# Linear attention and a top-2 expert layer in one kernel: the attention steps are put in another order, and each expert's weights are fetched in one burst

## The chip, the cores and the metric

The kernel runs on one core of a Trainium2 chip. The metric is the time on the device in microseconds (us), the median of several executions. In the text PE is TensorE (matrix products), DVE is VectorE, ACT is ScalarE, POOL is GpSimd and SP is SyncE. Each engine runs its own instructions strictly in program order and waits for the others by semaphores. POOL issues nearly all transfers here: those that convert 32-bit floats to bf16 on the way, and the indirect ones, which take a list of row numbers.

## What is computed

The reference has two parts. The first is linear attention on 8 batches of 8 heads with 576 positions of 64 numbers; the second is a layer of 8 experts that sees the 4608 outputs of the first as rows of 512 numbers.

```python
# attention, for every batch and head
phi = lambda x: np.where(x > 0, x, np.exp(x) - 1.0) + 1.0
q_p, k_p = phi(q), phi(k)
kv  = einsum('bhsd,bhse->bhde', k_p, v);   z = k_p.sum(axis=2)
num = einsum('bhsd,bhde->bhse', q_p, kv);  den = einsum('bhsd,bhd->bhs', q_p, z)[..., None] + 1e-6
x = (num / den)                            # to (4608, 512): the 8 heads of a position in one row

# router: two experts for each row
noisy = x @ w_gate + log1p(exp(x @ w_noise)) * noise        # (4608, 8)
top2, top2_w = the two largest of noisy in each row, and their softmax

# experts: w1[e] is 512 x 1024, w2[e] is 1024 x 512
for e in range(8):
    out[rows of e] += top2_w * (relu(x[rows of e] @ w1[e]) @ w2[e])
```

All inputs are 32-bit floats in HBM (q, k and v have 9.4 MB each, the experts' weights 33.6 MB); so is the output (9.4 MB).

## The kernel before

The batches are worked in four groups `g` of two. For each group there are loads of k, v and q, then these steps:

```python
def exp(self, g, t):               # ACT: two instructions, 128 x 2304 each
def phi(self, g, t, *parts):       # DVE: part 0 is max(x,0)+1 in place, parts 1 and 2 take the minimum with exp
def kv_mm(self, g, h):             # PE: half of k_p' v and of k_p' 1, into two tiles of ps_misc
def kv_ev(self, g, h):             # DVE: those two tiles to SBUF, masked
def kv_b1(self, g), kv_b2(self, g) # PE and ACT: kv times the router's weights, so that the logits come with num
def qt(self, g, *parts):           # PE transposes of q_p, ACT copies them out (5 parts)
def num(self, g, t):               # a third of the group: 3 of its 9 columns of rows
    ...                            # PE: dl = denominators and logits (24 small matmuls)
    ...                            # DVE: rden = 1/(den + 1e-6)
    for i in range(3):             # PE: num;  DVE: xr[g % 2] = num * rden (bf16 rows)
        ...
    ...                            # DVE: lwt = logits * rden
```

Routing works on a *unit*: some of the 9 columns of 128 rows of one group. Its three steps are chains of small DVE instructions, and a unit must have been counted before the next is placed (`carry` counts the rows that each expert has got). Dispatch then writes each finished row of 1152 bytes into the region of each of its two experts in HBM, one indirect transfer of 128 rows at a time.

```python
UNITS = [(0, 0, 3), (0, 3, 6), (0, 6, 9), (1, 0, 9), (2, 0, 9), (3, 0, 3), (3, 3, 9)]   # (group, first column, end)

def rt_a(self, u):                 # logits: sum lwt over the 8 heads, then softplus on ACT
    nc.vector.tensor_reduce(out=r["lg"], in_=_ap(self.lwt[:, c0], [[128, n], [1, 16], [16, 8]]), op=ALU.add, axis=AX.X)
    nc.scalar.activation(out=r["sp"], in_=r["lg"][:, :, 8:16], func=ACT.Exp)
    nc.scalar.activation(out=r["sp"], in_=r["sp"], func=ACT.Ln, bias=1.0, scale=1.0)
def rt_b(self, u): ...             # 15 DVE instructions: the two largest of 8; PE: ranks of the rows in each expert
def rt_c(self, u): ...             # 13 and more DVE instructions: softmax, row numbers posi, carry
def dispatch(self, u, a=0, z=9):
    for ci in range(c0 + a, min(c1, c0 + z)):
        for sl in range(2):
            self.nc.gpsimd.indirect_dma_start(out=self.x_sorted, out_offset=...posi[:, ci - c0, sl]..., in_=self.xr[g % 2][:, ci, :]...)
```

The order of the calls in `attention()` is the order on every engine. The middle of it, and its end:

```python
    for g, u in ((1, 3), (2, 4)):
        n = g + 1
        pa.exp(n, "q")
        pa.num(g, 0)
        pa.num(g, 1)
        pa.kv_mm(n, 0)
        pa.phi(n, "q")
        pa.num(g, 2)
        pa.kv_mm(n, 1)
        pa.kv_ev(n, 0)
        pa.rt_a(u)
        pa.kv_ev(n, 1)
        pa.kv_b1(n)
        pa.qt(n, 0)
        pa.rt_b(u)
        pa.kv_b2(n)
        if g == 1:
            pa.exp(3, "k")
            pa.phi(3, "k", 0)
        pa.rt_c(u)
        pa.qt(n, 1, 2, 3, 4)
        pa.dispatch(u, 0, 4)
        if g == 1:
            pa.load(3, "q")
        pa.dispatch(u, 4, 9)
        if g == 1:
            pa.phi(3, "k", 1, 2)
            pb.w_tiles(1)
            pb.w_load(1, 0, 1, 2, 3)
    # then the loads of expert 0's first rows (xt), num(3, ...), units 5 and 6, and the first products of expert 0
```

Buffers that set the order: three for k and q together (`A_kq`), two for v, two for exp (`A_e`), three PSUM tiles `ps_misc` for all of kv_mm, kv_b1, kv_b2 and qt, one PSUM tile `dl`, and two for the rows, `xr[g % 2]`.

The expert part takes the up to 1216 rows of an expert in blocks of 512, 512 and 192. While `mm1` of one block runs (rows times w1, relu), `mm2` of the block before (times w2), its gating and its output follow. A row that is the second visit of its token reads what the first visit wrote (gather), adds, and is written out (scatter), so the gather of a new expert waits until all scatters of the expert before have landed.

```python
    def interval(self, cur, prev, weights=()):
        ...                         # mm1(cur) in turn with mm2(prev, t) and scatter(prev, t)
        if cur and new and not cur["first"]:
            self.gather(cur)        # first block of an expert: behind the last scatter of the one before
        for e, i in weights:
            self.w_load(e, i)       # a quarter of an expert's weights: 1 MB of HBM, 0.5 MB of SBUF
# the loop over the blocks: two quarters in each interval until all are there
        loads = [(e, i) for e in range(2, E) for i in range(4)]
            todo, loads = loads[:2], loads[2:]
```

Of the kernel before, what the change touches and what calls it, by code (L numbers as in the profile page):

```python
# [15 lines left out]
P = 128  # L16
# [9 lines left out]
UNITS = [(0, 0, 3), (0, 3, 6), (0, 6, 9), (1, 0, 9), (2, 0, 9), (3, 0, 3), (3, 3, 9)]  # L26

ROUNDS = [(3, 512), (4, 768)]
# [76 lines left out]
class PhaseA:  # L105
# [36 lines left out]
    def exp(self, g, t):  # L142
        self.e[g, t] = self.ep.tile([P, 4, 9, P], BF16, name="e")
        for two in range(2):
            e, x = self._views(g, t, two)
            self.nc.scalar.activation(out=e, in_=x, func=ACT.Exp)  # L146
# [115 lines left out]
    def rt_a(self, u):  # L262
# [6 lines left out]
        nc.vector.tensor_reduce(  # L269
            out=r["lg"], in_=_ap(self.lwt[:, c0], [[128, n], [1, 16], [16, 8]]), op=ALU.add, axis=AX.X)  # L270
# [302 lines left out]
def attention(pa, pb, c, x_sorted, zrow):  # L573

    nc = pa.nc

    pa.exp(0, "k")
    pa.phi(0, "k")
    nc.vector.memset(zrow[:], 0.0)
    for e in range(E):  # L580

        for r0, n in ((1024, P), (1152, P)):
            nc.sync.dma_start(out=x_sorted[e * REGION + r0 : e * REGION + r0 + n, :], in_=zrow[0:n])
    pa.load(1, "q")
    pa.kv_mm(0, 0)
    pa.kv_ev(0, 0)
    pa.kv_mm(0, 1)
    pa.kv_ev(0, 1)
    pa.kv_b1(0)
# [3 lines left out]
    pa.qt(0, 0, 1, 2, 3, 4)  # L593
    pa.load(2, "k")
    pa.load(2, "v")
    pb.w_tiles(0)
    pb.w_load(0, 0, 1, 2, 3)
    pa.exp(1, "k")
    pa.num(0, 0)
    pa.rt_a(0)  # L600
    pa.phi(1, "k", 0)
    pa.rt_b(0)
    pa.phi(1, "k", 1)
    pa.rt_c(0)
    pa.dispatch(0)
    pa.num(0, 1)
    pa.rt_a(1)
    pa.phi(1, "k", 2)
    pa.rt_b(1)
    pa.kv_mm(1, 0)  # L610
    pa.rt_c(1)
    pa.dispatch(1)
    pa.load(2, "q")
    pa.exp(1, "q")
    pa.num(0, 2)
    pa.rt_a(2)
    pa.kv_ev(1, 0)
    pa.rt_b(2)
    pa.kv_mm(1, 1)
    pa.phi(1, "q", 0)  # L620
    pa.rt_c(2)
    pa.dispatch(2)
    pa.kv_ev(1, 1)
    pa.kv_b1(1)
    pa.phi(1, "q", 1, 2)
    pa.qt(1, 0)
    pa.kv_b2(1)
    pa.qt(1, 1, 2, 3, 4)
    pa.load(3, "k")
    pa.load(3, "v")  # L630
    pa.exp(2, "k")
    pa.phi(2, "k")
    for g, u in ((1, 3), (2, 4)):
        n = g + 1
        pa.exp(n, "q")
        pa.num(g, 0)
        pa.num(g, 1)
# [3 lines left out]
        pa.kv_mm(n, 1)  # L641
        pa.kv_ev(n, 0)
        pa.rt_a(u)
        pa.kv_ev(n, 1)
        pa.kv_b1(n)
        pa.qt(n, 0)
        pa.rt_b(u)
        pa.kv_b2(n)
        if g == 1:
            pa.exp(3, "k")  # L650
            pa.phi(3, "k", 0)
        pa.rt_c(u)
        pa.qt(n, 1, 2, 3, 4)
        pa.dispatch(u, 0, 4)
        if g == 1:
            pa.load(3, "q")
# [127 lines left out]
```

## Time and profile before

| what | value |
|---|---|
| median of 3 executions | 558.66 us (547.3 to 565.68) |
| span of the profiled execution | 556.6 us |
| busy: PE, DVE, ACT, POOL | 358.6, 214.2, 157.8, 266.9 us |
| transfers issued by POOL: share of the 16 engines' span | 56.4% (69.90 MB) |
| transfers issued by SP and ACT | 17.2% (12.68 MB) |
| read from HBM and written to it | 79.83 MB, 32.90 MB |
| dispatches, scatters, gathers (indirect, POOL) | 72, 80, 70, each about 1 us of POOL |

A page cuts the span into 40 slices of 13.9 us and gives each engine's busy share in tenths. A second part follows the chain of work that ended last backwards from the end. Other views list, for a stretch of time, the instructions of one engine with the idle time before each and what ended it, or count who waited for whom.

### The profile page before, as it was taken

How to read it: one execution, taken by the hardware profiler on the slowest of the kernel's cores; microseconds unless marked ns; L12 is line 12 of the kernel's file. 1: busy time of each engine (PE TensorE's matmuls, PEld its weight loads, DVE VectorE, ACT ScalarE, POOL GpSimd, SP SyncE). 2: the span in 40 equal slices, each digit the busy share in tenths (PEclk: the TensorE clock that was granted, in tenths of full speed). 3: DMA queues.
4: the chain of work that ended last, by engine and by line, in shares of the span. 5: the costliest groups of instructions: out<-in, count | busy, mean ns of one | idle time of the engine just before them, and what ended most of it. 6: DMA issues, size and time to landing. Idle time of an engine off the chain costs nothing.

```text
span 556.6 us, 7359 instructions
## 1 busy us (share of the span) xinstructions
PE 358.6 (64%) x2783; PEld 202.7 (36%) x2811; DVE 214.2 (38%) x548; ACT 157.8 (28%) x272; POOL 266.9 (48%) x289
## 2 busy tenths in 40 slices
PE   0432343562443127569999999359949975999980
PEld 0432332452333113324454454224424442454440
DVE  1438773856193166123335152023224233235130
ACT  2163318061222004113324324103402411424310
POOL 6023373006725613724585376068348474564660
PEclk9996555555556558969999999859969997999995
DMA  9999969202892331396499899969979794573640
GB/s 145 221 248 212 228 147 213 50 2 75 191 162 76 117 81 52 117 188 133 105 223 165 161 217 165 118 110 224 166 149 229 187 196 129 95 228 117 187 145 13
DMA packets 95311, 83.34 MB, mean 150 GB/s; under 512 B 58741, under 2 KB 81269, under 8 KB 95264
## 3 DMA queue, kind: packets, MB, share of 16 engines
q0 software_dynamic: 40448, 69.90, 56.4%
q1 hardware_dynamic: 53152, 12.68, 17.2%
q10 hardware_dynamic: 1664, 0.18, 0.4%
q8 instruction: 24, 0.39, 0.3%
q14 instruction: 23, 0.19, 0.1%
HBM read 79.83 MB, written 32.90 MB: 203 GB/s over the span
## 4 chain that ended last, share of the span: by engine, by line
PE 49%; DVE 14%; issue 13%; another core or an unknown queue 7%; ACT 7%; DMA 6%; POOL 2%; POOLq 0%; DVEq 0%; ACTq 0%
PE b L483 22%; PE b L472 21%; ACT e L146 4%; DVE e L156 3%; PE misc L170 2%; DMA out_dram<-y,si 2%; DVE xr L248 2%; PE num L226 2%; DMA kq<-in_q_dram 2%; DMA kq<-in_k_dram 2%; ACT pqt L219 1%; DVE kq L153 1%; DVE y L487 1%; DVE lwt L254 1%
## 5 line engine op out<-in xcount | busy, mean ns | idle before, releaser
L483 PE MATMUL b<-w,hT 128*128 128x512 bf16 (+1 forms) x624 | 156.5, 392 | 24.4 <-DVE y L487 23.0
L472 PE MATMUL b<-xt,w 128*128 128x512 bf16 (+3 forms) x756 | 149.5, 341 | 23.5 <-ACT hT L474 11.4
L474 ACT ACTIVATE hT<-b 128x512 bf16<-128x512 f32 (+3 forms) x192 | 95.5, 508 | 227.0 <-PE b L472 167.5
L487 DVE SCALAR_TENSOR_TENSOR y<-b,gate,L 128x512 f32<-128x512 f32 x70 | 50.8, 743 | 184.4 <-issue 64.6
L355 POOL DMA_INDIRECT x_sorted<-xr,posi x72 | 71.6, 994 | 104.2 <-ACT pqt L219 51.9
L497 POOL DMA_INDIRECT out_dram<-y,si x80 | 79.1, 989 | 63.1 <-DVE y L487 22.3
L472 PEld LDWEIGHTS <-w 128*128 128x128 bf16 x768 | 73.8, 100 | 95.7 <-issue 32.3
L455 POOL DMA_INDIRECT L<-out_dram,gi x70 | 71.2, 1016 | 73.9 <-DMA out_dram<-y,si 52.7
L483 PEld LDWEIGHTS <-hT 128*128 128x128 bf16 (+1 forms) x640 | 64.0, 102 | 97.3 <-issue 34.8
L226 PE MATMUL num<-kvbd,pqt 128*64 128x128 bf16 x288 | 21.3, 302 | 44.3 <-DVE xr L248 35.8
L226 PEld LDWEIGHTS <-pqt 128*64 128x64 bf16 x576 | 24.1, 156 | 70.4 <-issue 67.8
L146 ACT ACTIVATE e<-kq 128x2304 bf16<-128x2304 bf16 x16 | 33.0, 2124 | 31.7 <-issue 22.4
L446 DVE MEMSET L<- 128x512 f32 x70 | 34.0, 485 | 4.2 <-ACT hT L474 0.3
L170 PE MATMUL misc<-v,e 64*128 64x128 bf16 x288 | 19.5, 305 | 23.3 <-DVE e L156 19.6
L170 PEld LDWEIGHTS <-e 64*128 64x128 bf16 x576 | 20.2, 124 | 26.5 <-DVE e L156 19.6
L248 DVE TENSOR_TENSOR xr<-num,rden 128x512 bf16<-128x512 f32 x36 | 24.0, 689 | 15.0 <-remote 6.2
L153 DVE TENSOR_SCALAR kq<-kq 128x4608 bf16<-128x4608 bf16 x8 | 11.0, 1370 | 39.0 <-ACT e L146 39.0
L217 PE MATMUL misc<-ident,e 128*128 128x128 bf16 x144 | 16.9, 312 | 13.6 <-DVE e L156 10.7
L226 PE MATMUL dl<-kvbd,pqt 128*64 128x34 bf16 x288 | 11.1, 215 | 21.1 <-issue 12.3
L156 DVE TENSOR_TENSOR e<-e,kq 128x2304 bf16<-128x2304 bf16 x16 | 21.2, 1360 | 0.2
L490 DVE TENSOR_SCALAR y<-b,gate 128x512 f32<-128x512 f32 (+1 forms) x10 | 7.5, 750 | 34.4 <-PE b L483 19.0
L301 PE MATMUL dl<-A,ut 128*128 128x24 bf16 (+2 forms) x7 | 1.3, 190 | 29.4 <-DVE A L297 23.8
(91 smaller groups left out, 196.9 us busy)
## 6 DMA issues: line engine op xcount, KB each, us to landing
w<-in_moe_w_dram POOLq DMA_DIRECT2D x32, 512.0 KB
kq<-in_k_dram POOLq DMA_DIRECT2D x8, 576.0 KB
v<-in_v_dram POOLq DMA_DIRECT2D x8, 576.0 KB
kq<-in_q_dram POOLq DMA_DIRECT2D x8, 576.0 KB
x_sorted<-zrow SPq DMA_DIRECT2D x16, 144.0 KB
out_dram<-y,si POOLq DMA_INDIRECT x80
x_sorted<-xr,posi POOLq DMA_INDIRECT x72
L<-out_dram,gi POOLq DMA_INDIRECT x70
```

What stands on the lines that cost most here:

```text
L146: self.nc.scalar.activation(out=e, in_=x, func=ACT.Exp)
L156: nc.vector.tensor_tensor(out=e, in0=e, in1=x, op=ALU.min)
L170: nc.tensor.matmul(out=ps[j][:, i, cols], lhsT=e[half, hp, ci, :], rhs=r, start=(i == 0 and ci == 0 and rhs == "v"), stop=(i == 1 and ci = ...
L226: self.nc.tensor.matmul(out=out[half], lhsT=self.pqt[g, ci][:, hp, half], rhs=self.kvbd[g][:, j, hp, cols], start=start, stop=stop, skip_g ...
L248: nc.vector.tensor_tensor(out=_ap(xr[:, ci, 0:HD], [[64, 4], [256, 2], [1, 64]]), in0=_ap(ps, [[128, 4], [64, 2], [1, 64]]), in1=_ap(rden[ ...
L355: r = self.nc.gpsimd.indirect_dma_start(out=self.x_sorted, out_offset=bass.IndirectOffsetOnAxis(ap=self.r["posi", u][:, ci - c0, sl : sl + ...
L455: r = nc.gpsimd.indirect_dma_start(out=b["L"][t][0:m].bitcast(INT32), out_offset=None, in_=self.out.bitcast(INT32), in_offset=bass.Indirec ...
L472: nc.tensor.matmul(out=ps[:, 0:n], lhsT=w1[:, dc, fc * P : fc * P + P], rhs=b["xt"][:, dc, 0:n], start=(dc == 0), stop=(dc == 3))
L474: nc.scalar.activation(out=b["hT"][:, fc, 0:n], in_=ps[:, 0:n], func=ACT.Relu)
L483: nc.tensor.matmul(out=ps[0:m], lhsT=b["hT"][:, fc, t * P : t * P + m], rhs=w2[:, fc, :], start=(fc == 0), stop=(fc == 7))
L487: nc.vector.scalar_tensor_tensor(out=y[0:m], in0=ps[0:m], scalar=gate[0:m, tt : tt + 1], in1=b["L"][t][0:m], op0=ALU.mult, op1=ALU.add)
L497: r = nc.gpsimd.indirect_dma_start(out=self.out, out_offset=bass.IndirectOffsetOnAxis(ap=si[0:m, tt : tt + 1], axis=0), in_=b["y", t][0:m] ...
```

## The change

It is meant to let POOL, which issues every dispatch one after the other, start on them earlier, and to keep the weights out of the way of the transfers that an expert's beginning waits for. The parts are these.

1. **Units.** Groups 0, 1 and 2 are one routing unit of 9 columns each (group 0 was three units of 3); group 3 is 6 + 3 columns (it was 3 + 6). There are five units in place of seven.
2. **Dispatch directly behind its routing.** In the loop, rt_b, rt_c and the dispatch follow each other; the transposes `qt` that were in between come ahead of them or behind.
3. **Exponentials and loads ahead of need.** exp(1, k) starts before the transposes of group 0; exp(3, k) comes before the last transposes; the loads of q for groups 2 and 3 are issued well ahead of their exponentials (load(3, q) stood in the middle of a dispatch).
4. **The sum over the heads** in rt_a is three additions by halves in place of one strided reduction.
5. **The zero rows** that mark unused places are half as many, and come later.
6. **Weights in one burst.** All four quarters of the weights of expert e + 2 are loaded in the first interval of expert e, in place of two quarters in each of the first twelve intervals.

The diff, cut:

```diff
--- before.py
+++ after.py
@@ -23,9 +23,9 @@
 CAP = 1216
 T_CAP = 10
 
-UNITS = [(0, 0, 3), (0, 3, 6), (0, 6, 9), (1, 0, 9), (2, 0, 9), (3, 0, 3), (3, 3, 9)]
-
-ROUNDS = [(3, 512), (4, 768)]
+UNITS = [(0, 0, 9), (1, 0, 9), (2, 0, 9), (3, 0, 6), (3, 6, 9)]
+
+ROUNDS = [(1, 512), (2, 768)]
 REGION = N_TOK
 ROW_W = 576
 BIG = 1.0e6
... (exp takes parts, as phi does)
@@ -266,8 +267,11 @@
         tile_ = lambda name, shape, dt=FP32: self.rt.tile([P] + shape, dt, name=name)
         r = self.r
         r["lg"], r["sp"] = tile_("lg", [9, 16])[:, 0:n], tile_("sp", [9, E])[:, 0:n]
-        nc.vector.tensor_reduce(
-            out=r["lg"], in_=_ap(self.lwt[:, c0], [[128, n], [1, 16], [16, 8]]), op=ALU.add, axis=AX.X)
+
+        lw = lambda a, z: self.lwt[:, c0:c1, a:z, :]
+        for k in (4, 2):
+            nc.vector.tensor_tensor(out=lw(0, k), in0=lw(0, k), in1=lw(k, 2 * k), op=ALU.add)
+        nc.vector.tensor_tensor(out=r["lg"], in0=self.lwt[:, c0:c1, 0, :], in1=self.lwt[:, c0:c1, 1, :], op=ALU.add)
         nc.scalar.activation(out=r["sp"], in_=r["lg"][:, :, 8:16], func=ACT.Exp)
         nc.scalar.activation(out=r["sp"], in_=r["sp"], func=ACT.Ln, bias=1.0, scale=1.0)
 
@@ -573,92 +577,84 @@
 def attention(pa, pb, c, x_sorted, zrow):
 
     nc = pa.nc
-
     pa.exp(0, "k")
     pa.phi(0, "k")
-    nc.vector.memset(zrow[:], 0.0)      # and 16 transfers of 128 zero rows
     pa.load(1, "q")
     pa.kv_mm(0, 0)
+    pa.kv_mm(0, 1)
     pa.kv_ev(0, 0)
-    pa.kv_mm(0, 1)
     pa.kv_ev(0, 1)
+    pa.load(2, "v")
     pa.kv_b1(0)
     pa.kv_b2(0)
     pa.exp(0, "q")
     pa.phi(0, "q")
-    pa.qt(0, 0, 1, 2, 3, 4)
     pa.load(2, "k")
-    pa.load(2, "v")
-    pb.w_tiles(0)
-    pb.w_load(0, 0, 1, 2, 3)
-    pa.exp(1, "k")
+    pa.exp(1, "k", 0)
+    pa.qt(0, 0, 1)
+    pa.exp(1, "k", 1)
+
     pa.num(0, 0)
+    pa.qt(0, 2, 3, 4)
+    pa.phi(1, "k")
+    pa.load(2, "q")
+    pa.num(0, 1)
+    pa.kv_mm(1, 0)
+    pa.num(0, 2)
+    pa.kv_mm(1, 1)
+    nc.vector.memset(zrow[:], 0.0)
+    ...                                # 8 transfers of 128 zero rows, 8 of the marks of 64 rows
     pa.rt_a(0)
-    pa.phi(1, "k", 0)
+    pa.kv_ev(1, 0)
+    pa.kv_ev(1, 1)
+    pa.exp(1, "q")
+    pa.kv_b1(1)
     pa.rt_b(0)
-    pa.phi(1, "k", 1)
+    pa.phi(1, "q", 0)
     pa.rt_c(0)
-    pa.dispatch(0)
-    pa.num(0, 1)
-    pa.rt_a(1)
-    pa.phi(1, "k", 2)
-    pa.rt_b(1)
-    pa.kv_mm(1, 0)
-    pa.rt_c(1)
-    pa.dispatch(1)
-    pa.load(2, "q")
-    pa.exp(1, "q")
-    pa.num(0, 2)
-    pa.rt_a(2)
-    pa.kv_ev(1, 0)
-    pa.rt_b(2)
-    pa.kv_mm(1, 1)
-    pa.phi(1, "q", 0)
-    pa.rt_c(2)
-    pa.dispatch(2)
-    pa.kv_ev(1, 1)
-    pa.kv_b1(1)
+    pa.load(3, "v")
+    pa.dispatch(0, 0, 4)
     pa.phi(1, "q", 1, 2)
+    pa.load(3, "k")
+    pa.dispatch(0, 4, 9)
     pa.qt(1, 0)
     pa.kv_b2(1)
-    pa.qt(1, 1, 2, 3, 4)
-    pa.load(3, "k")
-    pa.load(3, "v")
+    pa.qt(1, 1)
     pa.exp(2, "k")
-    pa.phi(2, "k")
-    for g, u in ((1, 3), (2, 4)):
-        n = g + 1
+    pa.qt(1, 2, 3, 4)
+    for g in (1, 2):
+        n, u = g + 1, g
         pa.exp(n, "q")
         pa.num(g, 0)
+        pa.phi(n, "k")
+        if g == 1:
+            pa.load(3, "q")
+            pb.w_tiles(0)
+            pb.w_load(0, 0, 1, 2, 3)
         pa.num(g, 1)
         pa.kv_mm(n, 0)
         pa.phi(n, "q")
         pa.num(g, 2)
         pa.kv_mm(n, 1)
+        pa.qt(n, 0, 1)
+        pa.rt_a(u)
         pa.kv_ev(n, 0)
-        pa.rt_a(u)
         pa.kv_ev(n, 1)
         pa.kv_b1(n)
-        pa.qt(n, 0)
+        pa.qt(n, 2)
+        pa.kv_b2(n)
         pa.rt_b(u)
-        pa.kv_b2(n)
+        pa.rt_c(u)
+        pa.dispatch(u)
         if g == 1:
-            pa.exp(3, "k")
-            pa.phi(3, "k", 0)
-        pa.rt_c(u)
-        pa.qt(n, 1, 2, 3, 4)
-        pa.dispatch(u, 0, 4)
-        if g == 1:
-            pa.load(3, "q")
-        pa.dispatch(u, 4, 9)
-        if g == 1:
-            pa.phi(3, "k", 1, 2)
             pb.w_tiles(1)
             pb.w_load(1, 0, 1, 2, 3)
+            pa.exp(3, "k")
+        pa.qt(n, 3, 4)
 
     col = c["rowpos"]
     r1, r2 = pb.block(0, 0, 512, "r1", 0, True), pb.block(0, 512, 256, "r2", 0, True)
@@ -667,19 +663,20 @@
     pb.meta_load("r2", 512, 2, "read1")
     pb.xt_load(r2, "read1")
     pa.num(3, 0)
-    pa.rt_a(5)
     pa.num(3, 1)
-    pa.rt_b(5)
-    pa.rt_c(5)
-    pa.dispatch(5)
+    pa.rt_a(3)
     pa.num(3, 2)
-    pa.rt_a(6)
-    pb.mm1(r1, 0, 1, 2, 3)
-    pa.rt_b(6)
-    pb.mm1(r1, 4, 5)
-    pa.rt_c(6)
-    pa.dispatch(6)
-    pb.mm1(r1, 6, 7)
+    pa.rt_b(3)
+    pa.rt_c(3)
+    pa.dispatch(3)
+    pb.mm1(r1, 0)
+    pa.rt_a(4)
+    pb.mm1(r1, 1, 2)
+    pa.rt_b(4)
+    pb.mm1(r1, 3, 4)
+    pa.rt_c(4)
+    pa.dispatch(4)
+    pb.mm1(r1, 5, 6, 7)
     pb.meta("r1", c["cnt"][0][:], col[:, 0:4], code_of(0))
     pb.interval(r2, r1)
     pb.meta("r2", c["cnt"][1][:], col[:, 4:6], code_of(0))
@@ -731,7 +728,6 @@
         blocks = [pb.block(0, 768, CAP - 768, 0, 6, True)]
         for e in range(1, E):
             blocks += [pb.block(e, r, n, e, r // P) for r, n in ((0, 512), (512, 512), (1024, CAP - 1024))]
-        loads = [(e, i) for e in range(2, E) for i in range(4)]
         pb.meta_load(0, 0, T_CAP)
         pb.xt_load(blocks[0])
         for i, b in enumerate(blocks):
@@ -743,10 +739,10 @@
             if i == 0 or b["e"] != blocks[i - 1]["e"]:
                 e = b["e"]
                 pb.meta(e, c["carry"][:, e : e + 1], c["rowpos"][:], code_of(e))
-            todo, loads = loads[:2], loads[2:]
-            for e, part in todo:
-                if part == 0:
-                    pb.w_tiles(e, 1 if e < 6 else 0)
+            todo = []
+            if e + 2 < E and (i == 0 or b["e"] != blocks[i - 1]["e"]):
+                pb.w_tiles(e + 2, 1 if e + 2 < 6 else 0)
+                todo = [(e + 2, part) for part in range(4)]
             pb.interval(b, prev, todo)
             prev = b
         pb.interval(None, prev)
```

## Prediction

> **What bounds the kernel now.** I read the page's slices first, then POOL's instructions in order of time over the attention, then the chain of waits, then who waited for whom in the expert part, and last the busy time in one stretch per expert. The slices, of 13.9 us each:
>
> ```profile
> PE   0432343562443127569999999359949975999980
> DVE  1438773856193166123335152023224233235130
> POOL 6023373006725613724585376068348474564660
> PEclk9996555555556558969999999859969997999995
> DMA  9999969202892331396499899969979794573640
> ```
>
> Two halves with different limits. Up to slice 17 no engine is full: PE seldom over half, at half its clock, DVE full in single slices, the DMA engines full only to slice 6. That is a chain of waits, not an engine at its peak. From slice 18 PE is at 9 with holes at slices 25, 26 and 29, and the DMA engines are full up to slice 29 and not after. The next view is POOL's timeline; the columns are start, duration, instruction and, in brackets, its idle time just before and who ended that:
>
> ```profile
> 86.14 0.75 POOL L132 DMA_DIRECT2D kq<-in_k_dram  x1
> ...
> 127.73 2.09 POOL L355 DMA_INDIRECT x_sorted<-xr,posi  x1 [37.68 <-ACT pqt L219]
> ...
> 138.72 1.48 POOL L132 DMA_DIRECT2D kq<-in_q_dram  x2
> ...
> 170.90 1.03 POOL L355 DMA_INDIRECT x_sorted<-xr,posi  x1 [14.26 <-ACT pqt L219]
> ...
> 205.45 0.95 POOL L355 DMA_INDIRECT x_sorted<-xr,posi  x1 [11.99 <-issue]
> ...
> 220.80 0.96 POOL L355 DMA_INDIRECT x_sorted<-xr,posi  x1 [8.07 <-ACT hT L474]
> ```
>
> These are the first dispatches of groups 1 (127.73), 2 (170.90) and the two units of group 3. Inside a group they follow each other every 1.26 us, so group 2 and 3 with 36 dispatches need 45.5 us of POOL; they took 170.9 to 235.7, so 20 us of POOL waited for routing (11.99 + 8.07). Before that POOL stood 37.68 us with nothing to send. Between 127.73 and 138.72 stand eight dispatches ahead of the load of q for group 3, and its exponential waits for that load: "ACT e L146 <- issue: 22.4, 1, 22.4" in the list of waits, from 126.9 to 149.4.
>
> The expert part, POOL again, and then the busy time from each expert's first gather to the next (experts 1 to 6; columns: stretch, its length, busy us of PE, PEld, DVE, ACT, POOL with instruction counts, granted clock, share of the DMA engines, GB/s):
>
> ```profile
> 340.10 1.57 POOL L396 DMA_DIRECT2D w<-in_moe_w_dram  x2
> 341.97 1.04 POOL L497 DMA_INDIRECT out_dram<-y,si  x1 [0.30 <-DVE y L487]
> 343.32 0.96 POOL L497 DMA_INDIRECT out_dram<-y,si  x1 [0.30 <-issue]
> 364.61 1.04 POOL L455 DMA_INDIRECT L<-out_dram,gi  x1 [20.33 <-DMA out_dram<-y,si]
> ```
>
> ```profile
> 270.80:313.60 42.80, 42.27 (x212) 20.51 (x215) 12.94 (x26) 15.25 (x31) 25.19 (x26) 1.00 1.06 183
> 313.60:364.60 51.00, 39.51 (x203) 19.50 (x206) 12.74 (x26) 14.28 (x29) 24.88 (x26) 0.92 1.05 157
> 364.60:409.00 44.40, 36.34 (x173) 17.64 (x176) 12.66 (x26) 12.02 (x24) 25.03 (x27) 0.88 1.02 174
> 409.00:443.30 34.30, 30.05 (x141) 14.53 (x144) 12.66 (x26) 9.53 (x19) 23.24 (x24) 0.87 0.88 193
> 443.30:478.90 35.60, 26.65 (x131) 13.04 (x133) 12.53 (x26) 7.91 (x18) 19.98 (x21) 0.90 0.58 136
> 478.90:513.10 34.20, 33.90 (x174) 16.66 (x176) 12.54 (x26) 11.75 (x24) 19.86 (x21) 1.00 0.65 170
> ```
>
> Experts 1 to 3, with six quarters of weights each, take 42.8, 51.0 and 44.4 us; expert 4 with four and experts 5 and 6 with none take 34.2 to 35.6. The excess is the boundary: two quarters were queued just ahead of the last two scatters, so these land late and the next gather stands 10.75, 20.33 and 13.58 us, against 3.62, 2.21 and 2.17 us at the last three boundaries.
>
> **What the Trainium skill says.** "DMA: Bandwidth & Descriptors", section "Issuing engines are not separate DMA queues": all issuing engines' transfers run on the same 16 DMA engines and interleave. The trace agrees: POOL's own transfers take 56.4% of them and those of SP and ACT 17.2%, and a scatter that lands in about 2 us alone took 20 us behind weights. The same page, "Two DMAs through the same engine are not ordered": a transfer that reads what an earlier one wrote has to wait for its completion; that is the gather's wait, 52.7 us in six cases. "VectorE: DVE Perf Modes", "Rules for kernel authors", expects tensor_reduce at 1x only and advises restructuring; here the sum over 1152 elements took 2078 ns. "TensorE: Matmul & The Clock Gate", Part 1, tells of a half clock after an idle window; the granted clock was 0.5 over most of 46 to 213 us.
>
> **The change part by part.** *Routing.* A 3-column unit costs DVE 0.80 (sum) + about 3.0 (rt_b, from 47.2 to 50.2) + 1.5 (rt_c) = 5.3 us, three of them 15.9. One 9-column unit costs 3.6 (164.4 to 168.1) + 2.6 (125.0 to 127.6) and the new sum: additions of 384 and 144 elements take 548 and 308 ns, so about 0.16 us + 1 ns an element; 576 + 288 + 144 elements give about 1.5 us. Together 7.7, so 8 us of DVE less in group 0, and 0.6 us less in each of groups 1 and 2.
>
> *Group 0 to the first dispatch of group 1.* Up to phi(0, q), which ends at 36.5, nothing moves. Then I lay durations of the profile end to end in the new order: a num takes 3.3 us of DVE (0.18 + 0.30 + 3 x 0.69 + 0.55), a phi 4.0 (1.37 + 2 x 1.36), an exp 4.1 of ACT. Group 0's three nums with phi(1, k) among them end near 56, its routing near 70 (it contains 2.6 us for the second kv_mm, which needs a PSUM tile back that kv_ev releases). Dispatch of group 0 runs from 70 to 93; it used to begin at 53.8, and this is the one thing that comes later. Nothing waits for it. Group 1: num 76 to 79, phi(2, k) to 85, num, phi(2, q), num to 95, rt_a to 97, kv_ev, kv_mm and the two transposes ahead of rt_a's ACT work cost some 6 us, rt_b from 103, rt_c done near 109. So group 1's dispatch starts at 109 rather than 127.7.
>
> *Group 2.* Its q is loaded by 54, that of group 3 by about 102 (POOL is free of group 0 at 93), so the 22.4 us wait of the exponential goes. Three nums, two phis, rt_a, kv_ev and the wait for kv_mm, rt_b and rt_c are 10 + 8 + 1.5 + 6 + 3.7 + 2.6 = 32 us: dispatch of group 2 from 141 (POOL has ended group 1 and the weights of expert 1 at 136), against 170.9.
>
> *Group 3.* Its nums and first routing (3 x 3.3 + 1.2 + 3.5 + 2.3 = 17 us) lie beside the 22.8 us of group 2's dispatch, so POOL need not stop: 141 + 45.5 = 187 against 235.7, 49 us earlier. I don't believe all of it. During the same run of dispatches before, DVE's next instruction stood 12.2 us although all that it waited for seemed done ("another core or an unknown queue" in the chain, at 184.4, and again 12.15 us at 228.8). If that belongs to long runs of dispatches it comes back; I take off 12 us and keep 37.
>
> *Expert 0* and the first two blocks follow the last dispatch as before (35.1 us from 235.7 to the first gather at 270.8): no change. All four quarters of expert 2 now lie ahead of four scatters, but some 10 us before these are issued.
>
> *Experts 1 to 5.* Four quarters each. A quarter costs the DMA engines about 2.2 us: 0.88 x 34.3 = 30.2 us in expert 4, 0.58 x 35.6 = 20.6 and 0.65 x 34.2 = 22.2 in experts 5 and 6, so (30.2 - 21.4) / 4. Such an expert then asks for 30 us of the engines, under the 34.2 of PE, and the burst is over some 20 us before its last scatters. I expect 35 us for each: 175 against 42.8 + 51.0 + 44.4 + 34.3 + 35.6 = 208.1, a gain of 33 us. *Experts 6 and 7 and the end* (77.7 us) stay. *The zero rows*, 16 transfers of 144 KB, were beside compute; halving them is worth nothing.
>
> Sum: 556.6 - 37 - 33 = 487; plus 2 for the difference between the median and the profiled span gives 489. I add 5 us for orders that collide in ways I can't see: **494 us**.
>
> **The rivals.** First, the dispatches' standstill grows: runs of 18 without a pause now come three times in a row, with the nums of the next group needed inside each. Should 15 us be lost in each of the last two, the attention gains 15 rather than 37, and the time is 516. For it speaks the chain's 12 us pieces; against it, that group 1's run from 127.7 to 153.0 let six evictions of num through, one of them 2.3 us late. Second, the burst is a new blockade: the gathers of an expert's second block queue behind four quarters (9 us), and mm2 of that block waits. They are issued 14 us before they are needed, so I expect little; if 5 us came back in each of five experts the time would be 519. Third, the expert part is bound by the DMA engines' total and not by the boundary: then it needs (1.06 x 42.8 + 1.05 x 51.0 + 1.02 x 44.4 - 3 x 21.4) / 18 = 4.3 us for a quarter, 38.6 us for an expert, and 5 x 3.6 = 18 us come back: 512. Fourth, DVE holds up group 0 so that its late dispatch pushes everything: POOL has 16 us of slack there, so no.
>
> **Range and chances.** Without any standstill the sum is 556.6 - 49 - 33 + 2 = 477; with two of the rivals together it is near 535. I give 472 to 532 eight chances in ten. Runs of before spread over 547.3 to 565.7, so even the bad case is clear of it mostly: faster by over 2% 0.93, within 2% 0.04, slower by over 2% 0.03.
>
> **What would show it.** In POOL's timeline the first dispatches of groups 1 and 2 near 109 and 141, the last of all between 187 and 200, and no idle time over 3 us in between; the exponentials' 22.4 us wait gone. In the expert part, gathers of a new expert behind waits of 2 to 4 us, stretches of 35 us, and a DMA share near 0.88 in each of experts 1 to 5. Wrong would be: dispatches that start early but with PE and DVE still standing until the run ends, stretches over 38 us with short boundary waits (then total transfer is the limit), or DVE waits for gathers of second blocks.

## The result, and the profile after

The changed kernel takes 526.96 us (median of 4 runs, 520.5 to 531.7) against 553.62 us before: a ratio of 0.953, 95% interval 0.939 to 0.968. The gain is 4.7%; the prediction, 494 us, meant 11.6%. Both profiled executions, 556.6 and 521.9 us of span, are read below. First the slices of the changed kernel, 13.0 us each:

```profile
PE   0427435454363045399998899899999958999980
DVE  1437749358353084034233326116125206134240
POOL 6111128838707607534285685756655646664660
PEclk9998675565566558599999999999999987999995
DMA  9999855696472333376959599698699696763630
```

Counted from 0, PE is full from slice 17, and almost without holes up to slice 31. In slices 4 to 16 nothing is full steadily: the attention is still a chain of waits, and DMA is at 2 to 3 tenths in slices 12 to 16. POOL's timeline (start, duration, instruction, idle time before and who ended it) gives the first dispatch of each group or unit, and the first gather of expert 1:

```profile
74.16 1.06 POOL L359 DMA_INDIRECT x_sorted<-xr,posi  x1 [13.05 <-DMA x_sorted<-zrow]
113.48 1.02 POOL L359 DMA_INDIRECT x_sorted<-xr,posi  x1 [7.41 <-issue]
157.66 1.03 POOL L359 DMA_INDIRECT x_sorted<-xr,posi  x1 [15.98 <-ACT pqt L220]
195.22 0.96 POOL L359 DMA_INDIRECT x_sorted<-xr,posi  x1 [14.93 <-issue]
...
260.74 1.05 POOL L459 DMA_INDIRECT L<-out_dram,gi  x1 [6.06 <-DMA out_dram<-y,si]
```

The last dispatch ends at 217.7 us. Groups 1 and 2 come 14 and 13 us earlier than before, not 19 and 30, and ahead of group 2 and of group 3 POOL still stands 16.0 and 14.9 us without routed rows. DVE, which makes the routing, shows what it waited for while group 1 (113.5 to 138.6) and group 2 (157.7 to 180.3) were being dispatched:

```profile
139.95 0.18 DVE L242 TENSOR_SCALAR rden<-dl 128x24 f32<-128x24 f32 x1 [8.49 <-PE num L227]
...
171.19 0.18 DVE L242 TENSOR_SCALAR rden<-dl 128x24 f32<-128x24 f32 x1 [8.13 <-remote]
...
183.16 1.29 DVE L249 TENSOR_TENSOR xr<-num,rden 128x512 bf16<-128x512 f32 x2 [6.34 <-remote]
```

Each time DVE waits for a product of PE. It gets the first and the third 1.3 and 2.9 us after POOL's run of dispatches has ended, the second in the middle of group 2's run. Last, the stretches from one expert's first gather to the next, experts 2 to 5 (columns: stretch, length, busy us of PE, PEld, DVE, ACT, POOL, granted clock, DMA share, GB/s):

```profile
295.66:330.49 34.83, 33.28 (x171) 16.04 (x170) 12.57 (x26) 10.56 (x22) 23.25 (x25) 1.00 0.87 184
330.49:367.74 37.25, 35.80 (x184) 17.38 (x184) 12.57 (x26) 13.41 (x28) 23.32 (x24) 1.00 0.88 181
367.74:408.02 40.28, 40.28 (x207) 19.51 (x206) 12.63 (x26) 13.86 (x28) 23.10 (x25) 1.00 1.00 189
408.02:445.17 37.15, 29.03 (x141) 13.66 (x140) 12.46 (x26) 8.62 (x19) 23.11 (x25) 0.86 0.81 187
```

With expert 1 (34.92) they make 184.4 us. The boundaries wait 2.0 to 4.8 us instead of up to 20.3.

Where the 34.9 us less of span lie: attention (end of the last dispatch) 235.7 to 217.7, 18.0 gained; expert 0 (from there to the first gather) 35.1 to 43.0, 7.9 lost; experts 1 to 5 208.1 to 184.4, 23.7 gained; the rest 77.7 to 76.7. The trace of before is of an execution of 558.4 us, where the quickest took 547.3, so the gains of the stages may be too large by some us. The attention's hardly is: b_burst below, which has the old order of it, ends its last dispatch at 236.6 us in an execution of 533.0 us. Against the sum of the prediction (486.6): attention +19.0, expert 0 +7.9, experts 1 to 5 +9.4, rest -1.0.

### The profile page after: what moved, and what is told of

Same layout as the page of the kernel before. It is cut to its first block, busy times and chain, and to the rows that moved or that the text cites. A ratio compares the mean times of both kernels' runs of the same rounds, so it can differ in the third digit from the quotient of the medians.

```text
span 521.9 us, 7336 instructions
## 1 busy us (share of the span) xinstructions
PE 357.3 (68%) x2809; PEld 198.3 (38%) x2809; DVE 203.5 (39%) x500; ACT 155.8 (30%) x262; POOL 268.5 (51%) x289
## 5 line engine op out<-in xcount | busy, mean ns | idle before, releaser
L487 PE MATMUL b<-w,hT 128*128 128x512 bf16 (+1 forms) x640 | 154.6, 386 | 13.2 <-DVE y L491 10.2
L476 PE MATMUL b<-xt,w 128*128 128x512 bf16 (+3 forms) x768 | 152.2, 342 | 15.6 <-issue 9.7
L491 DVE SCALAR_TENSOR_TENSOR y<-b,gate,L 128x512 f32<-128x512 f32 x70 | 50.2, 740 | 165.4 <-DMA L<-out_dram,gi 100.9
L359 POOL DMA_INDIRECT x_sorted<-xr,posi x72 | 74.5, 1034 | 72.1 <-issue 41.9
L227 PEld LDWEIGHTS <-pqt 128*64 128x64 bf16 x576 | 22.5, 151 | 60.5 <-issue 58.1
L171 PE MATMUL misc<-v,e 64*128 64x128 bf16 x288 | 20.3, 303 | 31.5 <-DVE e L157 19.6
L220 ACT COPY pqt<-misc 128x1024 bf16<-128x1024 bf16 (+1 forms) x20 | 17.7, 933 | 61.0 <-PE misc L218 61.0
L249 DVE TENSOR_TENSOR xr<-num,rden 128x512 bf16<-128x512 f32 x36 | 23.9, 689 | 19.1 <-remote 12.2
L218 PE MATMUL misc<-ident,e 128*128 128x128 bf16 x144 | 16.7, 303 | 13.9 <-DVE e L157 13.8
L218 PEld LDWEIGHTS <-e 128*128 128x128 bf16 x144 | 14.2, 141 | 14.4 <-DVE e L157 14.0
```

Source lines behind the costliest of these rows:

```text
L171: nc.tensor.matmul(out=ps[j][:, i, cols], lhsT=e[half, hp, ci, :], rhs=r, start=(i == 0 and ci == 0 and rhs == "v"), stop=(i == 1 and ci = ...
L218: nc.tensor.transpose(tp[:, o : o + P], self.e[g, "q"][:, hp, ci, :], self.c["ident"][:])
L227: self.nc.tensor.matmul(out=out[half], lhsT=self.pqt[g, ci][:, hp, half], rhs=self.kvbd[g][:, j, hp, cols], start=start, stop=stop, skip_g ...
L359: r = self.nc.gpsimd.indirect_dma_start(out=self.x_sorted, out_offset=bass.IndirectOffsetOnAxis(ap=self.r["posi", u][:, ci - c0, sl : sl + ...
L476: nc.tensor.matmul(out=ps[:, 0:n], lhsT=w1[:, dc, fc * P : fc * P + P], rhs=b["xt"][:, dc, 0:n], start=(dc == 0), stop=(dc == 3))
L487: nc.tensor.matmul(out=ps[0:m], lhsT=b["hT"][:, fc, t * P : t * P + m], rhs=w2[:, fc, :], start=(fc == 0), stop=(fc == 7))
```

## Experiments

Times are medians beside runs of the kernel before on the same chip; chips differ, so ratios are compared. Executions of one kernel fall into a quick and a slow state: ratios use the quick ones alone, and since some traces are of executions up to 4% longer than the quickest, stage times of single traces are trusted to a few us only. "Experts 1 to 5" means their five stretches.

### 1. The two halves of the change, each alone

a_spread is the changed kernel without the burst, b_burst the kernel before with it:

```diff
-            if e + 2 < E and (i == 0 or b["e"] != blocks[i - 1]["e"]):
-                todo = [(e + 2, part) for part in range(4)]
+            todo, loads = loads[:2], loads[2:]
```

> The changed kernel with the weights of experts 2 to 7 spread again, two quarters behind each interval as before the change. Theory A (the burst removes the boundary waits and that is its whole worth, about 24 us by the stretches 208.1 against 184.4 us): boundaries of experts 2 to 4 wait 10 to 20 us again, experts 1 to 5 take about 208 us, the time is 547 to 555 us. Theory B (the boundary waits came from how the old attention left the expert part, not from the placement): experts 1 to 5 stay near 185 us and the time is 524 to 532 us.

> The kernel before with the burst alone. Theory A (the parts add): experts 1 to 5 go from 208 to about 184 us, the time is 527 to 533 us, so that the burst alone has nearly the whole gain and the new attention order brings little because what it wins it gives back in expert 0. Theory B (the parts need each other): 540 to 548 us.

Measured: a_spread 555.7 us against 556.8 of the kernel before, experts 1 to 5 215.4 us; b_burst 535.3 us, ratio 0.973 (0.953 to 0.993), experts 1 to 5 179.7 us. The boundary of expert 3 in POOL's timeline of a_spread:

```profile
354.93 1.05 POOL L459 DMA_INDIRECT L<-out_dram,gi  x1 [22.76 <-DMA out_dram<-y,si]
```

Theory A holds in both, with the time of b_burst 2 us above its range: the old boundary wait is back in full, and the burst alone has most of the gain. The burst was worth 28 us in the old order (208.1 to 179.7), near the 33 predicted. The new attention, by itself, gives nearly nothing: in the trace of a_spread the last dispatch ends 17.4 us earlier than in that of before (218.3 against 235.7), but the way from there to the first gather is 5.4 us longer and experts 1 to 5 are 7.3 us longer. b_burst also shows the burst's price in expert 0: from the last dispatch's start to the first gather 39.2 us against 36.1 before, with a boundary wait of 5.85 instead of 2.07 us, because four quarters now stand ahead of the last four scatters.

### 2. The burst behind the second block's gathers

```diff
             if not new:
                 self.gather(cur)
+                for e, i in weights:
+                    self.w_load(e, i)
+                weights = ()
...
-            if e + 2 < E and (i == 0 or b["e"] != blocks[i - 1]["e"]):
+            if e + 2 < E and i and i % 3 == 2 or i == 0:      # now the second block of an expert
```

> The changed kernel with the burst moved behind the gathers of an expert's second block. Theory C (the 9 us that experts 3 to 5 took over 35 us are gathers of the second block that queue behind four quarters): these DVE waits for gathers fall from 100.9 us to below 50 us, experts 1 to 5 take 175 to 178 us and the time is 515 to 520 us. Theory D (the expert part is bound by the total of transfers): the waits move elsewhere, experts 1 to 5 stay at 183 to 187 us, 525 to 529 us. Theory E (the later burst lands on the last scatters): boundary waits over 5 us, 530 us and more.

Measured: 533.0 us, ratio 0.966 (0.949 to 0.983), not told apart from the changed kernel's 0.953 to 0.954. DVE's waits for gathers 107.5 us, boundaries 3.0 to 5.2 us, experts 1 to 5 188.0 us. Theory C falls, as far as placement goes; the time is in E's range, though only two of the five boundary waits are over its 5 us.

### 3. Pauses in the runs of dispatches

a_pace adds, after every second column (four dispatches), two memsets on POOL; a_pace1 one; a_pace8 two after every eighth dispatch:

```diff
                 tc.add_to_no_dep_group("disp", r.ins)
+            if ci % 2 == 1:                       # a_pace8: ci % 4 == 3
+                for _ in range(2):                # a_pace1: range(1)
+                    self.nc.gpsimd.memset(self.idle[:], 0.0)     # 128 x 1024 bf16, 0.99 us
```

> The changed kernel with POOL doing two memsets of 1024 elements (about 2 us in all by the size of its other memsets) after every fourth dispatch. Theory F (PE crawls because POOL issues indirect transfers without a pause): the pauses break it, no evictions of num stand more than 3 us during dispatch of groups 1 and 2, the first dispatch of group 2 comes 5 to 9 us earlier (149 to 153 us) in spite of the pauses, and the first of unit 3 likewise follows the last of group 2 by under 10 us. Theory G (PE is late for its own order, its PSUM tiles or its half clock): the 8.5 us wait of DVE for PE stays, the first dispatch of group 2 is at 157 us or later, and the last dispatch comes 10 to 15 us later than 217.7 us.

> The changed kernel with one memset (about 1 us) after every fourth dispatch, half the pause of the run before. Theory F1 (it is the length of the unbroken run that makes PE crawl, so any short pause ends it): no DVE wait for PE over 3 us beside the dispatches of groups 1 and 2, and since POOL was the bound with the longer pauses, the last dispatch comes some 14 us earlier than there, at 197 to 202 us; time 503 to 509 us. Theory F2 (it is POOL's load on the whole, so the pauses have to be long): waits of 4 to 8 us come back, last dispatch at 208 us or later, time 515 to 522 us.

> The changed kernel with two memsets (2 us) after every eighth dispatch: as much pause as one memset after every fourth, but runs of 10 us. Theory F1 with a start of the crawl about 11 us into a run (as the standstills of before and after begin 11.5 to 12.7 us after the first dispatch of a run): no wait over 3 us, last dispatch at 197 to 202 us. Theory F3 (the crawl builds up earlier, and 8 are too many): DVE waits for PE of 3 to 6 us in each group, last dispatch at 204 us or later.

Measured: a_pace 521.5 us in one execution (before: 556.8). DVE's longest wait for PE's num beside the dispatches of groups 1 and 2 fell to the one of this line, and POOL stood nowhere over 2.4 us between 114.8 and the last dispatch:

```profile
159.70 1.29 DVE L250 TENSOR_TENSOR xr<-num,rden 128x512 bf16<-128x512 f32 x2 [1.51 <-PE num L228]
```

That is theory F, with group 2's first dispatch at 154.0, 1 us later than it said. POOL had become the bound, with 2 us of pause for every 5 us of dispatches, and still its last dispatch started 3 us earlier than without pauses (213.5 against 216.8). a_pace1, half the pause: last dispatch at 198.2, longest wait of DVE for a num 2.65 us, 505.1 us against 557.1 (497.1 to 511.7): theory F1, with its numbers. a_pace8, 505.7 us in one execution: waits of 6.0 and 3.2 us beside group 2's dispatch and none over 3 us beside group 1's, POOL idle 4.8 us ahead of unit 3, last dispatch at 208.5. Runs of eight are already too long (F3); the wait of 6.0 us began 5.4 us into the run, not 11.

### 4. Zero rows early, and the old order with pauses

a_pz writes the zero rows behind the first phi, as the kernel before did, and has the pauses of a_pace1. b_burst_pace1 is the kernel before with burst and pauses.

```diff
     pa.phi(0, "k")
+    nc.vector.memset(zrow[:], 0.0)
+    for e in range(E): ...          # the transfers of zero rows, moved here
```

> As the run with one memset after every fourth dispatch, and the zero rows written behind the first phi, as before the change. Theory H (group 0's dispatch really waits for the zero rows): its 13 us wait is gone, group 0 is dispatched from 61 to 65 us, group 1 then starts when its routing is done (107 to 111 us), the last dispatch comes 2 to 6 us earlier than with the late zero rows, time 499 to 506 us. Theory I (the zero rows only move in front of the loads, which are late by as much): no change of the last dispatch beyond 2 us.

> The kernel before with the burst and with one memset after every fourth dispatch: the old order of the attention without its standstills. Theory F says the two waits of 12 us of its groups 2 and 3 vanish, the last dispatch comes at 215 to 225 us instead of 235, the time is 515 to 526 us; the distance to the changed kernel with the same pauses (15 to 20 us) is what the new order of the attention is worth once PE does not crawl. If the old order reaches 510 us or less, the new order is worth nothing of its own.

Measured: a_pz 495.4 us, ratio 0.891 (0.882 to 0.899). The 13 us wait of group 0 is gone (its dispatch starts at 67.3), but group 1 starts at 109.6 and the last dispatch at 197.1, 1 us from a_pace1: theory I as far as the trace goes. The median is 10 us lower than a_pace1's, but two of a_pace1's four executions (497.1 and 501.0) lie only 1 to 9 us above four of a_pz's five (492.3 to 495.7); what remains these traces do not explain.

b_burst_pace1: 528.3 us, ratio 0.952 (0.943 to 0.960), last dispatch at 229.8. DVE's wait of 12.2 us for a num is gone (the longest is 3.6), but dispatch and time miss the expected 215 to 225 and 515 to 526 us: 6 us gained by the pauses, where the new order gains 19 (216.8 to 198.2). POOL's timeline tells why:

```profile
126.45 2.09 POOL L356 DMA_INDIRECT x_sorted<-xr,posi  x1 [34.81 <-ACT pqt L220]
```

In the old order POOL had nothing routed to send for 34.8 us, whatever PE did. The new order is right; but it put three runs of 18 dispatches without a break beside work of PE, where the old order had one, and behind the first two POOL had to wait for PE's products.

### 5. What in the dispatches does it

a_tiny puts a memset of 2 elements after every dispatch in place of the 1 us pauses. a_plain sends the same bytes as plain transfers to fixed places; rows are then not sorted and gathers fetch nothing, so only its attention is read.

```diff
-                r = self.nc.gpsimd.indirect_dma_start(out=self.x_sorted, out_offset=..., in_=self.xr[g % 2][:, ci, :]...)
+                r0 = (4 * sl + g) * REGION + ci * P
+                for h in (0, 64):
+                    r = self.nc.gpsimd.dma_start(out=self.x_sorted[r0 + h : r0 + h + 64, :],
+                                                 in_=self.xr[g % 2][h : h + 64, ci, :]...)
```

> Early zero rows as in the run before, and in place of a 1 us memset after every fourth dispatch a memset of 2 elements (about 0.1 us) after every one. Theory J (any other instruction of POOL between two dispatches ends the crawl, time is not needed): no DVE wait for PE over 3 us beside the dispatches of groups 1 and 2; POOL's pauses shrink from 16 to about 7 us in all; last dispatch 3 to 8 us earlier than with the longer pauses (189 to 194 us); 489 to 494 us. Theory K (it is the time without transfers being issued that counts): the standstills of 4 to 8 us come back, last dispatch at 203 us or later; 503 us or more.

> The changed kernel with each dispatch of 128 rows by index replaced by two plain transfers of 64 rows to fixed places, the same bytes from the same tile at about the same pace (each issue of a plain transfer takes 0.7 to 0.8 us); what follows works on rows in the wrong places and its gathers fetch nothing, so only the attention is read. Theory L (the transfers by index are what makes PE crawl): no DVE wait for PE over 3 us beside the runs of groups 1 and 2. Theory M (the traffic from xr to memory, or any uninterrupted issuing by POOL, does it): the waits of 4 to 8.5 us remain.

Measured: a_tiny 479.1 us, no wait of DVE for a num over 3 us beside the dispatches of groups 1 and 2, last dispatch at 185.4; a_plain 462.4 us (one execution), no such wait. But on this chip the kernel before took 525.5 us, not 550 to 557 as on the four others, and no trace of the unbroken kernel stood beside them. So both were run again, on another chip, with the changed kernel itself (a_same) and a_pz:

> The changed kernel itself, as the measure for the three that run beside it. If the standstill does not depend on the chip: DVE waits for PE of 4 to 8.5 us beside the dispatches of groups 1 and 2, POOL idle 13 to 17 us ahead of the dispatches of group 2 and of unit 3, ratio to the kernel before 0.94 to 0.97. If it belonged to the first chip alone, these waits are under 3 us here and the ratio is 0.90 to 0.92.

> Early zero rows and a memset of 2 elements after every dispatch, beside the unbroken kernel. Theory J (any instruction between two dispatches ends the crawl): no DVE wait for PE over 3 us beside groups 1 and 2, last dispatch 20 to 30 us earlier than in the unbroken kernel, ratio to it 0.93 to 0.95. Theory K (time without issuing is needed): waits as in the unbroken kernel, last dispatch within 8 us of it.

> Plain transfers of the same bytes to fixed places in place of the transfers by index, beside the unbroken kernel. Theory L (the transfers by index do it): no DVE wait for PE over 3 us, while the unbroken kernel shows 4 to 8.5 us on the same chip. Theory M (any traffic of POOL): waits of 4 us and more in both.

> Early zero rows and a 1 us memset after every fourth dispatch, beside the same with the tiny memsets. Theory J: 2 to 9 us slower than with the tiny ones (16 us of pauses against 7). Theory K: 8 us or more faster.

Measured beside a kernel before of 553.8 us: a_same 523.9 (ratio 0.954, 0.946 to 0.961), a_tiny_2 523.6 (0.953, 0.944 to 0.961), a_pz_2 497.5 (0.904, 0.894 to 0.915), a_plain_2 472.5 (one execution). The tiny memsets do nothing here; DVE in a_tiny_2:

```profile
140.76 0.18 DVE L243 TENSOR_SCALAR rden<-dl 128x24 f32<-128x24 f32 x1 [8.59 <-PE num L228]
```

Had only the first chip been read, theory J would have passed. K stands: it is time without issuing that counts. In a_tiny_2 there is hardly any more of it than without memsets: each falls into the gap of 0.3 us between two dispatches, which still come every 1.27 us. The memset of 1 us after every fourth makes that one step 2.10 us. The clearest view is PE's own timeline, at the same 24 small products of group 2's last num, group 1's dispatch running in both. In a_same, 24 matmuls in five portions:

```profile
131.66 0.29 PE L227 MATMUL dl<-kvbd,pqt 128*64 128x34 bf16 x4
132.30 0.36 PE L227 MATMUL dl<-kvbd,pqt 128*64 128x34 bf16 x6 [0.34 <-issue]
133.03 0.32 PE L227 MATMUL dl<-kvbd,pqt 128*64 128x34 bf16 x5 [0.37 <-issue]
133.76 0.35 PE L227 MATMUL dl<-kvbd,pqt 128*64 128x34 bf16 x6 [0.41 <-issue]
134.49 0.26 PE L227 MATMUL dl<-kvbd,pqt 128*64 128x34 bf16 x3 [0.38 <-issue]
```

and in a_pz_2, with the pauses, at once:

```profile
126.08 0.82 PE L228 MATMUL dl<-kvbd,pqt 128*64 128x34 bf16 x24
```

3.1 us against 0.8. PE waits for no other engine there ("issue"); it gets on by some five matmuls every 0.73 us. With the 16 products of num that follow it is 7.4 us (to 139.1) against 1.7, and DVE gets on at 140.3. The clock is not the reason: it was 0.50 in both stretches.

Beside group 2's dispatch the records look different. In the trace of the changed kernel the 24 small products of group 3's second num stand there at once, from 163.1 to 163.9 us, and the 16 larger ones until 165.2; but DVE gets the first result only at 171.19 (the line above) and the next at 176.13. Whether PE worked later than its records say or its signal came late the trace does not tell; the pauses take this wait away too (2.6 us in a_pz_2).

POOL's timeline of a_plain_2 shows that transfers as such are not the cause: 60 almost without a gap, one every 0.52 us.

```profile
148.66 21.78 POOL L361 DMA_DIRECT2D x_sorted<-xr  x42 [2.77 <-DMA w<-in_moe_w_dram]
170.87 9.34 POOL L361 DMA_DIRECT2D x_sorted<-xr  x18 [0.43 <-DMA x_sorted<-xr]
```

Beside this run PE works on: the first four results y of expert 0 come at 168.7 to 178.2 us, 3.2 us apart, while in a_same, beside the dispatches of units 3 and 4, none comes before 224.3, 6 us after the last of them. Nor does DVE wait over 2 us for a num between 100 and 165 us, though this says less: while the nums ran, the transfers had gaps of up to 3.8 us or had gone on for 6 us at most. Theory L, from one execution: it is the transfers by index, issued without a pause.

### 6. The expert part

Two placements and a pause, all on a_pz and on the chip of the 525.5 us:

```diff
-                todo = [(e + 2, part) for part in range(4)]                                  # a_pz_two
+                todo = [(e + 2, part) for part in ((0, 1) if i % 3 == 1 else (2, 3))]
+        nc.gpsimd.memset(self.idle[:], 0.0)     # a_pz_ep: after each block's gathers; half of it after every second scatter
```

> Early zero rows and 1 us pauses as before, and the four quarters of an expert's weights in two pairs: one behind the gathers of its first block, one behind those of its second. Theory N (the excess of experts 1 to 5 over 35 us is the one serial queue of POOL, in which a gather stands behind 13 us of weights): with two quarters ahead of the second block's gathers they land within 9 us, experts 1 to 5 take 175 to 178 us, time 487 to 492 us. Theory O (the queue is full in any order, or the last scatters stand behind the second pair): 183 to 190 us, 494 to 500 us.

> Early zero rows and 1 us pauses as before, and in the expert part a memset of 1 us after the gathers of each block and one of 0.5 us after every second scatter. Theory P (PE crawls in the expert part too, where POOL issues 10 to 14 transfers by index in a row): experts 1 to 5 go from 184 to 175 to 178 us, time 487 to 491 us. Theory N (their excess is the serial queue): no gain, 183 to 190 us, and the time is 494 to 500 us.

Measured: a_pz_two 494.7 us against 525.5, experts 1 to 5 187.8 us, boundaries up to 7.4 us. That fits theory O, but the four executions ran from 477.6 to 499.1 us and the trace is of one of 497.1, so N is not ruled out. a_pz_ep 519.8 us, ratio 0.990 (0.980 to 1.000), where a_tiny had 0.914 on the same chip: the pauses cost here; four stretches of 37 to 41 us and one of 56.2, in which one burst needed 30 us instead of 13 to 17 to land, which stays unexplained. Theory P is not confirmed, and neither theory had expected a loss.

The last two ask for the length of the pause and for the amount of weights. a_pz_halfw gives experts 4 to 7 the second weight matrix of the expert two before, not loaded again:

```diff
-                    self.nc.gpsimd.memset(self.idle[:], 0.0)                # a_pz_05: 0.55 us
+                    self.nc.gpsimd.memset(self.idle[:, 0:512], 0.0)
-                todo = [(e + 2, part) for part in range(4)]                  # a_pz_halfw, from expert 4
+                pb.w[e + 2] = (w1, pb.w[e][1])
+                todo = [(e + 2, part) for part in range(2)]
```

> Early zero rows, and after every fourth dispatch a memset of 512 elements (0.55 us) in place of 1024 (1 us). If what counts is any pause of some tenths of a us after four transfers: no DVE wait for PE over 3 us beside groups 1 and 2, last dispatch 5 to 8 us earlier than with 1 us (190 to 193 us against 197), ratio to the kernel before 0.88 to 0.895. If a pause has to outlast about 1 us: waits of 4 to 8 us are back, last dispatch at 205 us or later, ratio 0.92 or more.

> Early zero rows and 1 us pauses, and experts 4 to 7 work with the second weight matrix of the expert two before them, which is not loaded again: the bursts beside experts 2 to 5 are two quarters instead of four, that beside expert 1 is whole; the output is not the reference's. If the amount in POOL's queue causes the excess, the stretches of experts 2 to 5 are 34 to 35 us each (as that of expert 6 without a burst, 34.2) and that of expert 1 stays at 35; if it has another cause (pauses of PE, boundaries), they keep a mean of 36 to 37.5 us.

Measured: a_pz_05 512.3 us, ratio 0.937 (0.921 to 0.954), waits of 4.7 and 3.4 us, POOL idle 8.0 and 11.0 us ahead of group 2 and unit 3, last dispatch at 209.0: half a pause, about half the cure. a_pz_halfw, 492.1 us in one execution: DVE's waits for gathers 21.8 us instead of 75.2 in a_pz_2, but experts 2 to 5 38.2, 35.6, 35.4 and 35.2, mean 36.1 against 36.2 there. So, as far as single traces tell, neither the waits for gathers nor the amount set the excess; only one stretch of the four is far over 35. The 38.2 are this stretch (columns as above):

```profile
271.01:309.26 38.25, 34.76 (x164) 17.05 (x167) 12.73 (x26) 10.82 (x23) 21.60 (x22) 0.91 0.56 140
```

DMA share 0.56, clock 0.91: nothing is full, and PE's clock is halved for 7 us of it. Just before, from 277.8 to 292, POOL issued eleven transfers by index with 0.3 us between them. That looks like the same crawl; it is not shown there, and a_pz_ep, with pauses at these transfers, was not faster.

## Why the prediction was wrong, point by point

**The step that failed is the term for the standstill.** The prediction laid the attention end to end to 187 us, saw two standstills of 12 us in the profile of before, took off 12 us in all, and set the rest of the fear apart as its first rival. The term was 30.7 us (217.7 - 187). That it was the standstill, and not the sum of durations, is shown by a_pz_2, POOL again. Its last dispatch ends at 198.6, and from group 1 on 12 pauses lie in it, each of which adds 0.8 us; without these 10 us it is 189, near 187:

```profile
110.79 1.03 POOL L360 DMA_INDIRECT x_sorted<-xr,posi  x1 [7.24 <-issue]
...
146.59 1.02 POOL L360 DMA_INDIRECT x_sorted<-xr,posi  x1 [4.35 <-ACT pqt L221]
...
197.64 0.96 POOL L360 DMA_INDIRECT x_sorted<-xr,posi  x1 [0.30 <-issue]
```

The trace of before already had the standstill where it cost nothing, beside the second half of group 1's dispatch. There the 24 small products of group 2's last num took 6.6 us, from 144.1 to 150.7, while the exponential of q stood anyway; three of their six portions:

```profile
146.23 0.33 PE L226 MATMUL dl<-kvbd,pqt 128*64 128x34 bf16 x5 [1.13 <-issue]
147.65 0.30 PE L226 MATMUL dl<-kvbd,pqt 128*64 128x34 bf16 x4 [1.08 <-issue]
149.10 0.30 PE L226 MATMUL dl<-kvbd,pqt 128*64 128x34 bf16 x4 [1.15 <-issue]
```

- *Group 0 at 70:* 74.2. Its wait for the zero rows costs nothing, as predicted of both: a_tiny_2, with early rows, starts it at 68.0 and group 1 at 114.2, against 113.9 in a_same. The fourth rival was rightly dropped.
- *Group 1 at 109:* 113.5, near.
- *Group 2 at 141:* 157.7; 146.6 with pauses. Of the 16.7 us, 4.5 come from group 1 and 8.5 are DVE's wait at 139.95; the other 3.7 are not taken apart.
- *Group 3 hidden beside group 2's dispatch, POOL need not stop:* it stopped 14.9 us, because PE's nums of group 3 had to run inside that dispatch. With pauses it does not stop. The exponentials' wait of 22.4 us is gone, as predicted.
- *Expert 0 unchanged:* 43.0 instead of 35.1. Some 3 to 4 us are the burst ahead of its last scatters (5.85 against 2.07 us in b_burst; predicted as harmless "some 10 us before"). The other 4 to 5 us are the standstill again: beside units 3 and 4, 18 dispatches without a break, ACT gets PE's groups of four products 4.2 us apart (it starts on them at 206.6, 210.8, 215.0 and 219.2 us in the trace of the changed kernel), while each group's four matmuls take 1.0 us. In a_pz_2 the phase (from the start of the last dispatch) is 40.1 against 44.5 us in a_same.
- *Experts 1 to 5 at 35 us:* 184.4, then 183.3 in a_same and 179.7 in b_burst. The mechanism was right (boundaries short, DMA share 0.81 to 1.00 around the predicted 0.88), the size 5 to 9 us off. The second rival named the gathers behind the burst; but DVE's waits for gathers were 100.9 us in the trace of the changed kernel and 51.7 in a_same, with nearly the same stretches, and moving or halving the burst did not bring the 35 us. Halving it speaks against the third rival too, the total of transfers (whose sum gives 4.4 us for a quarter and 39 for an expert, not 4.3 and 38.6). What makes this excess stays open.
- *Experts 6 and 7, the end:* 76.7 for 77.7.

The first rival came true almost as written: 30 us lost leave 19 of the 49 us gained (the prediction wrote 15), and 18.0 were gained. The second, 5 us in each of five experts, came at 9.4 us in all, and 7.9 us were lost in expert 0, where no rival looked. 527 lies inside the range of 472 to 532, which allowed for such rivals; the middle value trusted an allowance copied from the old profile. What spoke against the first rival (six evictions passing in group 1's run) was the part of the run ahead of the load of q, up to 138.7 us; PE's portions begin at 142.5, 14.8 us after the first dispatch.

**A version that is faster than both:** the changed kernel with early zero rows and a pause of 1 us after every fourth dispatch, 0.891 (0.882 to 0.899) and 0.904 (0.894 to 0.915) of the kernel before on two chips, 495 to 498 us.

## What to carry to other kernels

When a reordering makes a queue of indexed transfers run without gaps, look in PE's timeline for matmuls that come in small portions with "issue" between them, or whose results reach the next engine several us after their record, before counting on what is to run beside it; a pause of 1 us after every four transfers took 26 us off here (a_tiny_2 523.6, a_pz_2 497.5; both have early zero rows). An allowance for a wait whose cause is not known should grow with what the change does to its trigger, not be copied from the old profile. And a remedy is tried beside the unmended kernel on the same chip: one of these looked like a cure where there was, it seems, no illness.

## What the runs showed of the hardware

- PE's products come late beside POOL's unbroken transfers by index. The Trainium skill ("SBUF — State Buffer", section "SBUF: two separate sides") says that PE never waits on another engine at the SBUF's ports. The measurement here, 24 matmuls in 3.1 instead of 0.8 us beside unbroken transfers by index, is a slowing all the same; no run shows that it lies at those ports.
- It depends on the pause: 0.1 us after each transfer, which leaves the pace at 1.27 us, does nothing, 0.55 us after four about half, 1 us after four nearly all. It depends, it seems, on the chip: a_tiny's DVE waited 8.6 us for a num on one and nowhere over 3 us on another, where the kernel before was 5% faster.
- Its cause is open. The skill ("Runtime: NRT & Kernel Launch", section "Instruction fetch mechanics") tells of instruction blocks of 16 KiB that each engine fetches by its own queue. The trace of the changed kernel has packets of 16384 bytes of one instruction queue, whose engine it does not name, at 122.2 and 145.2 us and none between, while PE crawls from 129 to 139. That neither supports nor excludes a late block, and no run tried it.
